# Attention with a key cache on one core: the second turn's keys transposed on TensorE, four steps of probabilities transposed by transfers, and a new order of all queues

## The chip, the cores and the metric

The kernel runs on one core of one Trainium2 chip. The metric is the device time of one execution in microseconds. A core has TensorE (matrix products, results into PSUM), VectorE and ScalarE (they copy out of PSUM and do the elementwise work), GpSimd (here only the identity matrix), and SyncE, which issues all transfers of this kernel, in one queue, SP: an instruction that waits there holds all that stand behind it.

## The reference

For 8 batches of 112 queries: q = x @ wq, with x of 8 x 112 x 640 and wq of 640 x 6144 (32 heads of 192); per batch and head scores = q @ k^T / sqrt(192) against 512 cached keys, p = softmax(scores), o = p @ v; then out = o @ wo, of 6144 x 640. All inputs and the output are bf16.

```
q = (x @ wq).reshape(B, Sq, H, Dh).transpose(0, 2, 1, 3)
scores = einsum("bhqd,bhkd->bhqk", q, k_cache) * Dh ** -0.5
p = softmax(scores)
o = einsum("bhqk,bhkd->bhqd", p, v_cache)
out = o.transpose(0, 2, 1, 3).reshape(B, Sq, H * Dh) @ wo
```

## The kernel before

The work goes in 16 turns: turn t takes one half of the heads (16) of one batch, first the lower half of all eight batches, then the upper. A turn has four steps of four heads; step n = 4t + s is the unit of softmax. Everything is unrolled, and the order on each engine is written out as text: `SP_WORK`, `PE_WORK`, `ACT_WORK`, `DVE_WORK`, one word an operation. `Plan.run` emits each list in its order, and before an operation waits for the semaphores of those it depends on (inputs ready, or a buffer or PSUM bank read out). So the order is fixed; only waits are found by the program.

The words on TensorE (the last number of most is the PSUM bank):

- X c: transposes of one chunk of 128 rows of x, five matmuls against the identity. K u: transposes of the keys of head u, six matmuls (line 477); the keys come untransposed as U lo.hi into `kn`, which lies in `wo_sb`. Before the change this is so in turn 0 alone; from turn 1 on K t on SP is one transfer of 3 MB that transposes on its way into `kt[t % 2]` (line 432). It waits until turn t - 2's scores have read that buffer.
- A m.lp and B m.lp: q for a pair of batches m and a pair of heads lp, two blocks (ten matmuls) and one block (five) of 224 columns (line 490). ScalarE copies them out (a, b) into places that `Q_PLACES` lists.
- S n: scores of step n (lines 521 to 538). VectorE makes the masked copies of q first (c, line 675), then scales and takes the maximum (m, line 685); ScalarE takes the exponent with its sum (e, line 695); VectorE inverts (r) and normalises (n, line 710).
- T n.j: transposes of p, eight matmuls (line 548), copied out by ScalarE (t n.0) and VectorE (t n.1). V n: the products with the values (lines 568, 581), copied out by ScalarE (v). `p_sb` holds two steps, so e of step n waits until p of step n - 2 has been read.
- O u.f.i: four matmuls each of o @ wo (line 597), added up by VectorE (p). In the last turns G (line 612) and L (line 627) take their place, and F (line 638) transposes the result of a batch, which ScalarE copies out (o) and Z stores.

On SP stand besides: X and W (x and wq), V t.lo (half a turn's values, 1.5 MB, two buffers and at the start a third in `wo_sb`), Y (wo), Z (stores). W of the upper half waits until q of the lower half has been made from the same columns; V waits until its buffer's last values were used.

## Time and profile before

| | us |
|---|---|
| median of three runs | 459.64 (459.57 to 460.03) |
| the profiled execution's own time | 460.54 |
| its span, first to last instruction | 458.7 |
| TensorE busy | 438.4 (96%) |
| VectorE busy | 360.8 (79%) |
| ScalarE busy | 347.3 (76%) |

The span is shorter than the execution's own time by what lies around the program. A group of instructions is named by its line, its engine and its tiles, output first. Busy time of TensorE runs to the modelled end of each matmul, and matmuls overlap, so the distance from one piece to the next tells more of their cost than their durations. The granted clock is the share of full speed that TensorE was given. For a transfer the view of a source line gives how long SP was held by its issue, the start of the issue, and the time from there to its landing.

### The profile page before, as it was taken

The page shows a single profiled execution, that of the slowest core. Times are in us where ns is not written, and L with a number is a line of the kernel's source. Part 1 is how long each engine was busy: PE and PEld are TensorE (multiplying, and loading weights), DVE is VectorE, ACT ScalarE, POOL GpSimd, SP SyncE. Part 2 cuts the span into 40 slices and gives each one's busy share as a digit, 9 for nine tenths or more (in the row PEclk, how much of TensorE's full clock was granted, in tenths as well). Part 3 has the DMA queues.
Part 4 walks back from the last instruction along what each step waited for, and adds up shares of the span by engine and source line. Part 5 has one row for each costly group of instructions (what it writes and reads, how often), then busy time and mean ns, then how long its engine had stood idle before and what let it go on. Part 6 is the DMA issues. An engine that isn't in the chain of part 4 may idle for free.

```text
span 458.7 us, 14942 instructions
## 1 busy us (share of the span) xinstructions
PE 438.4 (96%) x6307; PEld 399.2 (87%) x6307; DVE 360.8 (79%) x1165; ACT 347.3 (76%) x787; POOL 0.7 (0%) x6
## 2 busy tenths in 40 slices
PE   4999899999999999999999999997999999999996
...
PEclk9899999999999999999999999999999999999999
...
GB/s 278 372 350 224 241 327 352 237 306 287 260 215 247 362 275 214 308 243 331 206 337 209 309 235 326 300 189 368 225 274 260 281 287 261 219 253 222 178 14 51
DMA packets 234321, 119.63 MB, mean 261 GB/s; under 512 B 185744, under 2 KB 234256, under 8 KB 234256
## 3 DMA queue, kind: packets, MB, share of 16 engines
...
q14 instruction: 16, 0.13, 0.1%
HBM read 70.35 MB, written 1.15 MB: 156 GB/s over the span
## 4 chain that ended last, share of the span: by engine, by line
PE 87%; ACT 4%; DMA 4%; DVE 3%; issue 1%; SPq 0%; ACTq 0%
PE ps L490 18%; PE ps L597 17%; PE ps L581 12%; PE ps L548 10%; PE ps L536 7%; PE ps L568 7%; PE ps L521 6%; PE ps L523 6%; DMA wq_sb<-in_wq_dram 2%; ACT p_sb L695 2%; DMA vt<-in_v_cache_dram 2%; PE ps L612 1%; DVE s_sb L685 1%; PE ps L627 1%; ACT acc_q L650 1%
## 5 line engine op out<-in xcount | busy, mean ns | idle before, releaser
L695 ACT ACTIVATE p_sb<-s_sb,nmx 112x512 bf16<-112x512 f32 x256 | 183.1, 717 | 42.3 <-DVE s_sb L685 40.7
L685 DVE TENSOR_SCALAR_CACHE_REDUCE s_sb<-ps 112x512 f32<-112x512 f32 x256 | 172.9, 684 | 41.3 <-PE ps L538 16.9
L490 PE MATMUL ps<-xT_sb,wq_sb 128*128 128x224 bf16 x960 | 110.0, 262 | 2.7 <-DMA wq_sb<-in_wq_dram 0.9
L597 PE MATMUL ps<-oT_sb,wo_sb 128*128 128x224 bf16 x840 | 95.0, 259 | 0.8 <-ACT acc_q L650 0.4
L490 PEld LDWEIGHTS ps<-xT_sb,wq_sb 128*128 128x128 bf16 x960 | 88.6, 99 | 7.4 <-DMA wq_sb<-in_wq_dram 1.9
L710 DVE TENSOR_SCALAR p_sb<-p_sb,rinv 112x512 bf16<-112x512 bf16 x256 | 84.6, 349 | 3.2
L597 PEld LDWEIGHTS ps<-oT_sb,wo_sb 128*128 128x128 bf16 x840 | 77.1, 98 | 2.5 <-issue 0.7
L650 ACT ACTIVATE acc_q<-ps 128x224 bf16<-128x224 f32 (+1 forms) x128 | 55.9, 447 | 24.6 <-PE ps L490 19.8
L650 ACT ACTIVATE pT_sb<-ps 128x896 bf16<-128x896 bf16 x64 | 58.3, 911 | 13.0 <-PE ps L548 12.8
L548 PE MATMUL ps<-ident,p_sb 112*128 112x112 bf16 x1024 | 65.3, 213 | 0.1
L650 ACT ACTIVATE oT_sb<-ps 128x672 bf16<-128x672 f32 x64 | 46.5, 727 | 18.5 <-PE ps L581 16.2
L548 PEld LDWEIGHTS ps<-ident,p_sb 112*128 112x128 bf16 x1024 | 57.7, 98 | 2.5 <-DVE p_sb L710 0.7
L581 PE MATMUL ps<-pT_sb,vt 128*128 128x112 bf16 x992 | 59.5, 213 | 0.0
L581 PEld LDWEIGHTS ps<-pT_sb,vt 128*128 128x128 bf16 x992 | 49.8, 98 | 4.9
L695 ACT ACTIVATION_READ_ACCUMULATOR p_sb<-s_sb,nmx 112x1 f32 x256 | 49.2, 192 | 0.0
L650 DVE COPY pT_sb<-ps 128x896 bf16<-128x896 bf16 x64 | 39.7, 620 | 12.0 <-PE ps L548 11.2
L568 PEld LDWEIGHTS ps<-pT_sb,vt 128*64 128x64 bf16 x992 | 27.3, 109 | 16.8 <-ACT p_sb L695 7.2
L568 PE MATMUL ps<-pT_sb,vt 128*64 128x112 bf16 x992 | 36.2, 215 | 5.4 <-DVE p_sb L710 2.6
L521 PE MATMUL ps<-kt,acc_q 128*112 128x256 bf16 x128 | 35.2, 275 | 1.3 <-DVE kt L650 0.7
L523 PE MATMUL ps<-kt,acc_q 128*112 128x256 bf16 x128 | 34.9, 273 | 0.0
L521 PE MATMUL ps<-kt,qh 128*112 128x256 bf16 x128 | 34.9, 272 | 0.0
L523 PE MATMUL ps<-kt,qh 128*112 128x256 bf16 x128 | 34.9, 272 | 0.0
...
## 6 DMA issues: line engine op xcount, KB each, us to landing
...
wo_sb<-in_wo_dram SPq DMA_DIRECT2D x4, 1920.0 KB, 13.5
wq_sb<-in_wq_dram SPq DMA_DIRECT2D x7, 960.0 KB, 10.7
...
```

The source lines that it names most:

```text
L490: mm = e.matmul(ps[:, bank, j * S2:(j + 1) * S2], wq_sb[:, dc, c0:c0 + 128], xT_sb[:, dc, bp * S2:(bp + 1) * S2], start=(dc == 0), stop=(d ...
L521: e.matmul(ps[0:SQ, 2 * j, hs], ev, ktb[:, :, 0, cs(i)], start=(h == 0), stop=False, skip_group_check=True)
L523: mm = e.matmul(ps[0:SQ, 2 * j + 1, hs], od, ktb[:, :, 2, cs(i)], start=(h == 0), stop=False, skip_group_check=True)
L536: m1 = e.matmul(ps[0:SQ, 2 * j, hs], ev, ktb[0:64, :, 1, cs(i)], start=False, stop=True, skip_group_check=True)
L548: mm = e.transpose(psb[:, bank, c:c + SQ], p_sb[:, (4 * n + 2 * j + h) % 8, q * 128:(q + 1) * 128], ident[0:SQ, 0:SQ])
L568: mm = e.matmul(ps[64 * h:64 * h + 64, b0 + j, SQ:2 * SQ], vtb[:, h0 + 2 * j + h, d0:d0 + 64], pT(j, h, q), start=(q == 0), stop=(q == 3))
L581: mm = e.matmul(ps[:, b0 + j, 2 * h * SQ:(2 * h + 1) * SQ], vtb[:, h0 + 2 * j + h, d0:d0 + 128], pT(j, h, q), start=(q == 0), stop=(q == 3))
L597: mm = e.matmul(ps[:, bank, j * S2:(j + 1) * S2], wo_sb[:, KU * (u % 2) + k, m * 128:(m + 1) * 128], oT_sb[:, u % NO, k, :], start=(k == 0 ...
L650: return e.activation(dst, src, ACTF.Copy) if eng == "ACT" else e.tensor_copy(dst, src)
L685: return e.tensor_scalar(s_sb[:, a, :].rearrange("p (e c) -> p e c", e=2), ps[0:SQ, 2 * j:2 * j + 2, h * 256:(h + 1) * 256], -scale, None, ...
L695: return e.activation(p_sb[:, k, :], s_sb[:, a, :], ACTF.Exp, bias=nmx[:, k:k + 1], scale=-1.0, accum_out=rsum[:, k:k + 1])
L710: return e.tensor_scalar(p_sb[:, k, :], p_sb[:, k, :], rinv[:, k:k + 1], None, op0=ALU.mult)
```

## The change

Turn 1's keys are loaded untransposed too (U1.0.8 and U1.8.16, each once turn 0's keys have left those places of `kn`), and 16 more K words on TensorE transpose them; the copies go into `kt[1]`. The transposing transfer K1 is gone. K3, which takes `kt[1]` next, also waits for these copies.

D n products of the identity with itself (20 ahead of the first X, 8 ahead of the first A and B) go into a PSUM bank that nobody reads.

In steps 58 to 61 T and its two copies are gone. P n, a transfer on SP, transposes the four heads' p from `p_sb` into a part of `wq_sb` that is free once the last q has been made; V n reads it there, and e of step n + 2 waits for its landing instead of T.

The orders of all four lists and `Q_PLACES` are new: among others the head's transfers, Y0.1 now behind V2.0, V4.0 behind K5, W1.0.2 ahead of V5.0, W1.6.2 behind V7.0, Y1.0 behind V10.0, and the stores with Z2 behind Z6.

```diff
--- before.py
+++ after.py
@@ -17,238 +17,241 @@
...
 SP_WORK = """
-X0.0.2 W0.0.1 U0.4 W0.1.1 W0.2.2 X1.2.4 X2.4.7 U4.8 W0.6.2 W0.4.2 U8.16 V0.0 V0.8
-K1
-K2 V1.0 V1.8 Y0.0 V2.0
-K3 V2.8 Y0.1 V3.0
-K4 V3.8 V4.0
-K5 V4.8 W1.4.2 W1.2.2 V5.0 W1.0.2
+X1.2.4 X0.0.2 W0.1.1 W0.0.1 U0.0.4 W0.2.2 U0.4.8 W0.6.2 U0.8.16 W0.4.2 U1.0.8 X2.4.7 V0.0 V0.8 U1.8.16
+K2 V1.0 V1.8 Y0.0 V2.0 Y0.1
+K3 V2.8 V3.0
+K4 V3.8
+K5 V4.0 W1.2.2 V4.8 W1.4.2 W1.0.2 V5.0
 K6 V5.8 V6.0
-K7 V6.8 W1.6.2 V7.0
+K7 V6.8 V7.0 W1.6.2
 K8 V7.8 V8.0
 K9 V8.8 V9.0
-K10 V9.8 Y1.0 V10.0
+K10 V9.8 V10.0 Y1.0
 K11 V10.8 Y1.1 V11.0
 K12 V11.8 V12.0
 K13 V12.8 V13.0
 K14 V13.8 V14.0
-K15 V14.8 V15.0 V15.8 Z1 Z2 Z0 Z5 Z3 Z4 Z6 Z7
+K15 V14.8 P58 P59 V15.0 P60 P61 V15.8 Z3 Z0 Z1 Z4 Z6 Z2 Z5 Z7
 """
 PE_WORK = """
-X1.4 X0.6 A0.0.6 B0.0.4 K0.6 B0.1.5 A0.1.7 K2.3 K3.0 K1.2 A0.3.6 X2.5
-S0 A0.2.7 K6.0 B0.3.4 K5.5 X4.0 X3.1 X5.7 B0.7.6 B0.2.5 K7.2 K4.0 B0.6.7
-S1 B1.2.7 B1.3.6 B1.6.7 A0.6.6 K11.0 K8.1 A0.7.7 T0.0.4 K12.1 B0.5.6 X6.0 A0.4.7 K9.0 K15.3 A0.5.6 K10.5 B0.4.7 K13.4
-A1.6.6 B1.0.7 T0.1.5
...
-S44 V42.4 A6.2.6 A6.5.7 T43.0.4 T43.1.5
...
-S59 V57.4 O13.1.0.7 O13.1.1.7 O13.1.2.7 O13.1.3.7 F1.6 O13.1.4.7 O13.1.5.7 T58.0.4 T58.1.5 F2.6
-S60 V58.4 O12.2.0.7 O13.0.0.6 O12.2.1.7 O12.2.2.7 O13.0.1.6 O13.0.2.6 O13.2.0.7 O13.2.1.7 T59.0.4 T59.1.5 O13.2.2.7
-S61 V59.4 F0.6 G0.0.7 G0.1.7 G0.2.7 G1.0.6 G1.1.6 T60.0.4 G0.3.7 T60.1.5
-S62 V60.4 G1.2.6 G1.3.6 O13.3.0.7 O13.3.1.7 O13.3.2.7 T61.0.4 T61.1.5 F5.6
-S63 V61.4 G2.0.7 G2.1.7 G2.2.7 F4.6 G2.3.7 T62.0.4 T62.1.5 L0.0 V62.4 F3.6 T63.0.0 L1.0 T63.1.1 L0.1 L1.1 V63.2 L2.1
-L2.0 L3.0 L3.1 F6.5 F7.4
+D0.20.3 X3.5 X2.6 X1.4 X0.2 D1.8.3 B0.1.5 A0.1.6 A1.1.7 A0.0.6 B0.0.5 K0.0.1 K0.3.3 K0.2.0 K0.1.1 A1.0.6
+S0 B0.3.5 A0.2.6 B1.3.7 K0.5.5 B0.2.4 K0.4.0 A0.3.6 K0.6.1 B0.6.7 K0.7.6 A0.6.7
+S1 K0.11.5 A0.7.6 B0.7.7 T0.0.4 K0.12.5 K0.13.1 B0.4.7 A0.4.6 K0.10.0 B0.5.7 K0.8.1 K0.9.3 K1.1.0 K0.14.2 K0.15.4
+A0.5.6 X4.3 K1.5.4 X5.7 K1.7.2 T0.1.5 B1.0.6
+S2 V0.4 B1.6.7 K1.4.0 T1.0.4 T1.1.5 K1.2.6
+S3 V1.4 A1.6.7 K1.0.0 T2.0.4 K1.3.5 K1.10.1 A1.7.6 K1.6.7 T2.1.5 K1.8.6
+S4 V2.4 B1.2.6 K1.9.1 K1.11.0 A1.5.7 B1.7.6 X6.0 K1.14.2 B1.1.7 K1.12.3 K1.15.5 K1.13.4
+S5 A1.2.6 T3.0.4 A3.0.7 A2.0.6 T3.1.5
+S6 V3.4 A1.3.6 T4.0.4 T4.1.5 A3.7.7 B1.5.6 V4.4 A2.6.7 T5.0.4 T5.1.5
+S7 V5.4 A1.4.6 A2.5.7 B1.4.6 T6.0.4 T6.1.5
+S8 V6.4 A2.2.6 A3.3.7 T7.0.4 T7.1.5
...
+S40 B5.7.7 T38.1.5 O7.3.0.6 O7.3.1.6 B5.3.7 V38.4 A5.5.7 T39.0.4 O7.3.2.6 T39.1.5
+S41 V39.4 A6.1.6 T40.0.4 O7.0.0.7 T40.1.5 O7.0.1.7 O7.0.2.7 O8.3.0.6 O8.3.1.6 O8.3.2.6
...
+S43 V41.4 B6.0.7 O8.1.2.6 O8.1.3.6 O8.1.4.6 O8.1.5.6 A6.2.7 T42.0.4 T42.1.5
+S44 V42.4 B6.1.6 A6.0.7 T43.0.4 T43.1.5 A6.5.6
...
+S57 V55.4 O11.3.0.7 O11.3.1.7 O11.0.0.6 T56.0.4 O11.3.2.7 O11.0.1.6 O11.0.2.6 T56.1.5
+S58 V56.4 B7.7.6 O12.3.0.7 O12.3.1.7 O12.1.0.6 O12.1.1.6 O12.3.2.7 O12.1.2.6
+S59 F1.7 O12.1.3.6 O12.1.4.6 T57.0.4 O12.0.0.7 T57.1.5 O12.1.5.6 O12.0.1.7 O12.0.2.7 V57.4 F2.6
+S60 O13.1.0.7 O13.1.1.7 O13.0.0.6 O13.0.1.6 O13.0.2.6 O13.1.2.7 O13.1.3.7 O13.1.4.7 O12.2.0.6 O12.2.1.6 O13.1.5.7
+O12.2.2.6 V58.4 F3.7 O13.3.0.6 O13.3.1.6 O13.3.2.6 F0.7
+S61 V59.4 O13.2.0.7 O13.2.1.7 O13.2.2.7 G0.0.6 G0.1.6 G0.2.6 G0.3.6 G1.0.7
+S62 G1.1.7 G1.2.7 G1.3.7 G2.0.6 V60.4
+S63 F4.7 G2.1.6 G2.2.6 V61.4 G2.3.6 L0.0 T62.0.4 T62.1.5 L0.1 L1.1 T63.0.0 T63.1.1 V62.4 L1.0 V63.2 F6.4 L2.0 L3.0
+L2.1 L3.1 F5.7 F7.5
 """
 ACT_WORK = """
-x1 a0.0 b0.0 b0.1 a0.1 k1
-e0.0 a0.3 e0.1 e0.2 a0.2 b0.3 k5 b0.2 x3 k7 e0.3 b0.7 b0.6 b1.2 b1.3
...
-e63.0 v61 e63.1 t62.0 o4 e63.2 e63.3 v62 o3 t63.0 v63 o6 o7
+x3 x1 b0.1 a0.1 a0.0 b0.0 k0.1 a1.0 a1.1
+e0.0 b0.3 e0.1 a0.2 b0.2 b1.3 k0.5 a0.3 b0.6 k0.7 a0.6 e0.2 e0.3 k0.11
+e1.0 a0.7 b0.7 t0.0 b0.4 e1.1 k0.13 e1.2 a0.4 k0.9 b0.5 k0.15 k1.1 a0.5 e1.3 k1.7 k1.5 b1.0
+e2.0 v0 e2.1 t1.0 b1.6 e2.2 e2.3
+e3.0 v1 a1.6 e3.1 k1.3 e3.2 a1.7 t2.0 e3.3
+e4.0 b1.2 e4.1 k1.11 v2 a1.5 b1.7 e4.2 k1.9 k1.15 b1.1 e4.3 k1.13 a1.2
...
+e58.0 b7.7 e58.1 e58.2 e58.3 v56 o1
+e59.0 t57.0 e59.1 o2 e59.2 e59.3 v57
+e60.0 e60.1 o3 e60.2 v58 e60.3 o0
+e61.0 e61.1 v59 e61.2 e61.3
+e62.0 e62.1 e62.2 e62.3 v60 o4
+e63.0 e63.1 v61 e63.2 e63.3 t62.0 t63.0 v62 v63 o6 o5 o7
 """
 DVE_WORK = """
-x0 k0 k2 c0 k3
-m0.0 m0.1 x2 m0.2 k6 m0.3 x5 x4 c1 r0.0 k4
...
-m63.0 n62.1 r62.1 m63.1 n62.2 m63.2 n62.3 g2 r63.0 n63.0 t62.1 n63.1 m63.3 r63.1 n63.2 n63.3 t63.1 l0 l1
+x0 x2 k0.0 k0.3 k0.2 c0
+m0.0 m0.1 r0.0 m0.2 m0.3 k0.4 c1 k0.6 n0.0
+m1.0 m1.1 n0.1 r0.1 m1.2 m1.3 k0.10 n0.2 n0.3 k0.12 r1.0 n1.0 k0.14 k0.8 x4 c2 n1.1 x5 t0.1 r1.1 n1.2 n1.3
+m2.0 c3 m2.1 m2.2 k1.4 m2.3 t1.1 c4 r2.0
+m3.0 m3.1 n2.0 k1.2 n2.1 m3.2 r2.1 k1.0 k1.10 n2.2 n2.3 r3.0 c5 m3.3 t2.1 n3.0 k1.8 n3.1
...
+m59.0 m59.1 c60 r58.1 n58.2 t57.1 p12.1 m59.2 n58.3 r59.0 m59.3 n59.0 n59.1 p12.0 r59.1 n59.2 n59.3
+m60.0 p13.0 m60.1 c61 p12.2 p13.1 c62 m60.2 r60.0 n60.0 m60.3 n60.1 r60.1 n60.2
+m61.0 m61.1 n60.3 p13.3 m61.2 m61.3 c63 r61.0 p13.2 n61.0 n61.1 r61.1 n61.2 n61.3
+m62.0 g0 m62.1 m62.2 m62.3 g1 r62.0 n62.0 n62.1 r62.1
+m63.0 n62.2 m63.1 m63.2 m63.3 n62.3 g2 r63.0 n63.0 n63.1 r63.1 n63.2 n63.3 t62.1 t63.1 l0 l1
...
@@ -360,6 +363,7 @@
...
+        wq_flat = wq_sb[:].rearrange("p a b -> p (a b)")
         wo_flat = wo_sb[:].rearrange("p a b -> p (a b)")
...
@@ -375,14 +379,17 @@
...
         v_home = [0, 1, 2] + [(i + 1) % 2 for i in range(3, len(v_units))]
-        x_piece, wq_piece, kn_piece = {}, {}, {}
+        x_piece, wq_piece, kn_piece, by_dma = {}, {}, {}, []
         for kind, *a in work["SP"]:
+            if kind == "P":
+                by_dma.append(a[0])
             if kind == "X":
...
             elif kind == "U":
-                kn_piece.update({u: ("KN", *a) for u in range(*a)})
+                kn_piece.update({(a[0], u): ("KN", *a) for u in range(a[1], a[2])})
+        kn_turns = sorted({t for t, _ in kn_piece})
...
@@ -399,10 +406,11 @@
...
-        def load_kn(lo, hi):
-            def emit(e):
-                return e.dma_start(kn[:, lo:hi, :], k_cache[0, lo:hi].rearrange("u (r q) d -> r u (q d)", q=4))
-            add("SP", ("KN", lo, hi), [], emit, f"mKN{lo}", 16)
+        def load_kn(t, lo, hi):
+            def emit(e):
+                return e.dma_start(kn[:, lo:hi, :], k_cache[t, lo:hi].rearrange("u (r q) d -> r u (q d)", q=4))
+            old = [("KT", t - 1, u) for u in range(lo, hi)] if t else []
+            add("SP", ("KN", t, lo, hi), old, emit, f"mKN{t}_{lo}", 16)
...
@@ -421,7 +429,7 @@
...
             else:
-                old = [("KT", i) for i in range(HU)] + ([("PVm", 4, 1), ("PVm", 5, 1)] if u else [])
+                old = [("KT", *i) for i in kn_piece] + ([("PVm", 4, 1), ("PVm", 5, 1)] if u else [])
             add("SP", ("WO", half, u), old, emit, f"mWO{u}", 16)
...
@@ -431,6 +439,7 @@
...
             old = [("St", step_of(t - 2, s), 3) for s in range(4)] if t > 1 else []
+            old += [("evK", t - 2, u) for u in range(HU)] if t - 2 in kn_turns else []
             add("SP", ("K", t), old, emit, f"mK{t % 2}", 16)
...
@@ -445,13 +454,24 @@
...
             old = [("PVm", step_of(v_units[j][0], v_units[j][1] // 4 + s), 1) for j in old for s in range(2)]
-            old += [("KT", u) for u in range(HU)] if v_home[i] == 2 else []
+            old += [("KT", *i) for i in kn_piece] if v_home[i] == 2 else []
             add("SP", ("V", t, lo), old, emit, f"mV{v_home[i]}", 16)
...
             add("SP", ("OUT", b), [("oout", b)], emit, f"mOUT{b % DC}", 16)
+
+        def p_spare(n):
+            return wq_flat[:, by_dma.index(n) * 16 * SQ:(by_dma.index(n) + 1) * 16 * SQ].rearrange("p (c s) -> p c s", c=16)
+
+        def p_transposes(n):
+            k = 4 * n % 8
+
+            def emit(e):
+                return e.dma_start_transpose(p_spare(n), p_sb[:, k:k + 4, :].rearrange("p a c -> p (a c)"))
+            old = [d for m in range(NM // 2, NM) for lp in range(LP) for d in q_both(m, lp)]
+            add("SP", ("P", n), [("norm", n, i) for i in range(4)] + old, emit, f"mP{n % 2}", 16)
...
@@ -471,13 +491,21 @@
...
-        def k_transposes(u, bank):
+        def k_transposes(t, u, bank):
             def emit(e):
...
                 return mm
-            add("PE", ("KT", u), [kn_piece[u]], emit)
-            take(("KT", u), bank, ("KT", u), [("evK", u)])
+            add("PE", ("KT", t, u), [kn_piece[t, u]], emit)
+            take(("KT", t, u), bank, ("KT", t, u), [("evK", t, u)])
+
+        def idle_products(i, n, bank):
+            def emit(e):
+                for _ in range(n):
+                    mm = e.matmul(ps[:, bank, 0:128], ident[:, :], ident[:, :], start=True, stop=True)
+                return mm
+            add("PE", ("D", i), [], emit)
+            take(("D", i), bank, ("D", i), [])
...
@@ -523,7 +551,7 @@
...
                     return mm
-                add("PE", ("Sm", n, j), [("qc", n)] + ([("evK", 4 * s + i) for i in range(4)] if t == 0 else [("K", t)]),
+                add("PE", ("Sm", n, j), [("qc", n)] + ([("evK", t, 4 * s + i) for i in range(4)] if t in kn_turns else [("K", t)]),
                     emit)
...
@@ -558,7 +586,7 @@
...
             def pT(j, h, q):
-                return pT_sb[:, j, h, q * SQ:(q + 1) * SQ]
+                return p_spare(n)[:, 4 * (2 * j + h) + q, :] if n in by_dma else pT_sb[:, j, h, q * SQ:(q + 1) * SQ]
...
@@ -570,7 +598,8 @@
...
-            add("PE", ("PVt", n), [("evPT", n, 0), ("evPT", n, 1), ("V", t, 8 * (s // 2))], rests)
+            ready = [("P", n)] if n in by_dma else [("evPT", n, 0), ("evPT", n, 1)]
+            add("PE", ("PVt", n), ready + [("V", t, 8 * (s // 2))], rests)
             for j in range(2):
...
@@ -654,9 +683,9 @@
...
-        def ev_k(eng, u):
-            copy(eng, ("evK", u), [("KT", u)], kt[0][:].rearrange("p a m c -> p (a m) c")[:, :, u * 128:(u + 1) * 128],
-                 psb[:, bank_of["KT", u], 0:768].rearrange("p (c r) -> p c r", c=6))
+        def ev_k(eng, t, u):
+            copy(eng, ("evK", t, u), [("KT", t, u)], kt[t][:].rearrange("p a m c -> p (a m) c")[:, :, u * 128:(u + 1) * 128],
+                 psb[:, bank_of["KT", t, u], 0:768].rearrange("p (c r) -> p c r", c=6))
...
@@ -694,7 +723,8 @@
...
                                     accum_out=rsum[:, k:k + 1])
-            add(eng, ("exp", n, i), [("smax", n, i)] + ([("PT", n - 2, i // 2)] if n > 1 else []), emit)
+            old = [] if n < 2 else [("P", n - 2)] if n - 2 in by_dma else [("PT", n - 2, i // 2)]
+            add(eng, ("exp", n, i), [("smax", n, i)] + old, emit)
...
@@ -711,7 +741,8 @@
...
         def ev_pt(eng, n, j):
-            copy(eng, ("evPT", n, j), [("PT", n, j)] + ([("PVm", n - 1, j)] if n else []),
+            old = [("PVm", w, j) for w in range(n) if w not in by_dma][-1:]
+            copy(eng, ("evPT", n, j), [("PT", n, j)] + old,
                  pT_sb[:, j, :, :].rearrange("p h c -> p (h c)"), psb[:, bank_of["PT", n, j], 0:8 * SQ])
...
@@ -775,10 +806,11 @@
...
         bank_of = {(k + "T", *a[:-1]): a[-1] for k, *a in work["PE"] if k in "XK"}
-        loads = {"X": load_x, "W": load_wq, "U": load_kn, "V": load_v, "K": load_k, "Y": load_wo, "Z": store}
+        loads = {"X": load_x, "W": load_wq, "U": load_kn, "V": load_v, "K": load_k, "Y": load_wo, "Z": store,
+                 "P": p_transposes}
         for kind, *a in work["SP"]:
             loads[kind](*a)
-        on_pe = {"X": x_transposes, "K": k_transposes, "A": lambda *a: q_fill("a", *a), "B": lambda *a: q_fill("b", *a),
+        on_pe = {"D": idle_products, "X": x_transposes, "K": k_transposes, "A": lambda *a: q_fill("a", *a), "B": lambda *a: q_fill("b", *a),
                  "S": scores, "T": transposes, "V": values, "O": o_sums, "G": o_six, "L": o_last, "F": o_final}
...
```

336 lines of the change are left out of this document (155 added, 181 removed), and 16 rows, old and new, of the table Q_PLACES.

## The prediction

> **What bounds the kernel now.** I read the page first (shares, slices), then a table of stretches, then the order of the instructions at the head and at the one dip in the middle, then single transfers.
>
> ```profile
> span 458.7 us, 14942 instructions
> PE 438.4 (96%) x6307; PEld 399.2 (87%) x6307; DVE 360.8 (79%) x1165; ACT 347.3 (76%) x787; POOL 0.7 (0%) x6
> ...
> PE   4999899999999999999999999997999999999996
> ...
> PEclk9899999999999999999999999999999999999999
> ```
>
> TensorE is the bound nearly everywhere; what it loses lies in the first slices, at one dip (slice 28) and at the end. The stretches say how much (columns: length, busy time of PE, PEld, DVE, ACT, POOL, granted clock, DMA share, GB/s):
>
> ```profile
> 0.00:16.30 16.30, 9.77 (x79) 8.31 (x80) 2.79 (x7) 4.80 (x8) 0.70 (x6) 0.90 0.91 305
> 16.30:73.30 57.00, 53.79 (x713) 47.71 (x711) 39.43 (x124) 43.98 (x103) 0.00 (x0) 1.00 1.17 302
> 73.30:312.00 238.70, 235.36 (x3388) 214.46 (x3386) 204.75 (x665) 189.86 (x435) 0.00 (x0) 1.00 1.16 273
> 312.00:318.00 6.00, 3.40 (x56) 2.92 (x54) 4.04 (x14) 3.18 (x10) 0.00 (x0) 1.00 1.06 374
> ...
> 432.40:455.00 22.60, 22.29 (x417) 20.64 (x414) 14.24 (x46) 14.62 (x31) 0.00 (x0) 1.00 0.20 67
> 455.00:458.70 3.70, 0.00 (x0) 0.00 (x0) 0.00 (x0) 0.68 (x1) 0.00 (x0) 1.00 0.26 78
> ...
> 8.30:11.70 3.40, 1.53 (x17) 1.11 (x15) 0.56 (x1) 0.55 (x2) 0.00 (x0) 1.00 1.06 382
> 11.70:15.10 3.40, 3.40 (x29) 3.08 (x28) 1.00 (x3) 0.90 (x2) 0.00 (x0) 0.50 1.07 370
> ```
>
> To 16.3, where the scores of step 0 begin, PE works 9.8 of 16.3 us, and from 11.7 to 15.1, after a stretch with 1.53 us of work in 3.4, its clock is halved. The last 3.7 us hold no matmul. The dip at 312 loses 2.6 us.
>
> **The price of one word of the order.** Matmuls overlap, so I price by the distance to the next piece, as the chain of waits gives it (start, us, what):
>
> ```profile
> 2.32 8.65 DMA wq_sb<-in_wq_dram
> ...
> 29.49 0.67 PE ps L477 x12
> 30.16 0.96 PE ps L490 x10
> ...
> 39.89 0.51 PE ps L568 x16
> 40.41 0.89 PE ps L581 x16
> ...
> 423.92 0.79 PE ps L548 x16
> ```
>
> A key transpose of one head (K, six matmuls) is 0.67 / 2 = 0.34 us; A is 0.96 and B, half of it, 0.48; V is 0.51 + 0.89 = 1.40; T is 0.79 / 2 = 0.40; O, four matmuls of A's width, 0.38; a matmul of G or L I price like one of T, 49 ns.
>
> **TensorE work.** Added: 16 K, 16 x 0.34 = +5.4 us. Removed: two T in each of steps 58 to 61, 8 x 0.40 = -3.2 us. The 20 + 8 identity products I cost at nothing: their cover is the wait for the first transfers, below; without it, at half clock (183 ns for 224 columns, below, so some 0.1 us for 128) they would cost 2.8. Net +2.2 us, on the bound engine: the change must win that back from waits.
>
> **Head, to the scores of step 0.** The rows (start, us, then what; behind them single transfers, by issue time and by time to landing):
>
> ```profile
> 5.88 2.75 PE L490 MATMUL ps<-xT_sb,wq_sb 128*128 128x224 bf16 x15 [0.63 <-DVE xT_sb L650]
> ...
> 14.64 0.33 DVE L675 COPY qh<-acc_q 64x672 bf16<-64x672 bf16 x1
> ...
> 15.24 0.55 DVE L650 COPY kt<-ps 128x768 bf16<-128x768 bf16 x1
> ...
> 16.35 0.27 PE L521 MATMUL ps<-kt,acc_q 128*112 128x256 bf16 x1
> ...
> 73.38 0.28 PE L521 MATMUL ps<-kt,acc_q 128*112 128x256 bf16 x1
> ...
> L411 SPq DMA_DIRECT2D wq_sb<-in_wq_dram x1: 1074/1074/1074, 2.9 to 2.9; - x1
> DMA to landing us min/median/max: 10.7/10.7/10.7
> ```
>
> By the shapes, 320 + 480 + 768 + 480 = 2048 KB are queued up to the piece that lands at 2.32 + 8.65 = 10.97, and the next 960 KB land at 2.9 + 10.7 = 13.6: 2.64 us more. In the new order the last piece that step 0 needs, the keys U0.0.4, has 320 + 320 + 480 + 480 + 768 = 2368 KB up to it, so it lands at 10.97 + 320 / 960 x 2.64 = 11.9. Then one K (0.34), three copies of keys on VectorE (3 x 0.55) and the two copies of qc (2 x 0.33), with some 0.2 for handing over: S0 at 14.8 instead of 16.35. Up to there the new order has done 4 X, 4 A, 2 B, 4 K, the old 3 X, 3 A, 2 B, 4 K: 0.96 + 0.28 (an X is five transposes at 56 ns) = 1.24 us more. The gain is 1.55 + 1.24 = 2.8 us. Bounds: 1.2, if the keys land so late that S0 stays at 16.35; 4.3, if they land with the 2048 KB at 10.4 and hand over at once.
>
> The 15 matmuls at 5.88 took 2.75 us, against 0.96 for ten later on, or 1.44 for fifteen: half clock, 1.3 us; the halved stretch lost 1.7 more. The Trainium skill, page "TensorE: Matmul & The Clock Gate", section "Part 1: The HAM clock gate", says that the clock is halved by default, is released after one busy window of about 3.4 us, and comes back halved after an idle one; the trace agrees, with 0.50 for 3.4 us behind a poor window. By that rule alone, identity products from 1.5 us on would save 1.3 + 1.7 = 3.0 us. I don't add this to the 2.8: with the full clock PE waits for the same pieces, so the row of the transfer decides; by the rule the sum would be 0.2 lower.
>
> **S0 to S7 (16.35 to 73.38, 57.0 us).** By the prices above and 1.54 for an S (the start of one to the next word), the old order has 7 S, 17 A, 16 B, 12 K, 4 X, 12 T, 5 V: 51.7 us, so 5.3 are waits and stretching. The new has 7 S, 15 A, 13 B, 28 K, 3 X, 12 T, 5 V: 53.4 us. What it queues in front (X0 to U1.8.16, 320 x 2 + 960 x 4 + 480 + 768 x 2 + 1536 x 5 = 14176 KB) would land at 10.97 + (14176 - 2048) / 960 x 2.64 = 44.3; the K that needs its last piece stands 5 us behind S3, which comes 7.7 + 11.4 + 4.9 us of work and some 2 of waits after S0: near 46. So transfers stay just ahead, with under 2 us of margin; that is the cover, and beyond it each us late is a us of stall. The copies of the 16 heads fall on engines with room on average:
>
> ```profile
> L650 ACT ACTIVATE kt<-ps 128x768 bf16<-128x768 bf16 x7 | 5.7, 811 | 2.0 <-PE ps L477 2.0
> L650 DVE COPY kt<-ps 128x768 bf16<-128x768 bf16 x9 | 5.0, 553 | 11.3 <-PE ps L477 11.2
> ...
> L650 ACT ACTIVATE acc_q<-ps 128x448 bf16<-128x448 f32 x64 | 34.2, 539 | 11.1 <-PE ps L490 9.4 <-PE ps L538 1.5
> L650 ACT ACTIVATE acc_q<-ps 128x224 bf16<-128x224 f32 x64 | 22.3, 354 | 13.5 <-PE ps L490 10.3 <-PE ps L538 2.6
> ```
>
> ScalarE gets 8 x 0.81 and loses 3 x 0.54 + 3 x 0.35 and one X copy (0.7): 43.98 + 3.1 = 47.1 us; VectorE 39.43 + 8 x 0.55 - 0.5 = 43.4. I keep the 5.3 us of waits (bounds 3.2, PE's idle time in the stretch, and 9.3, worked out below). S7 then begins at 14.8 + 53.4 + 5.3 = 73.5, where it began before, with 0.8 us less work left.
>
> **From S7 on.** The work left falls from 375.5 to 374.7. The old order spends 454.95 - 73.38 - 375.5 = 6.1 us of waits here. The largest:
>
> ```profile
> 316.30 0.58 PE L568 MATMUL ps<-pT_sb,vt 128*64 128x112 bf16 x16 [2.60 <-DVE p_sb L710]
> ...
> L445 SPq DMA_DIRECT2D vt<-in_v_cache_dram x1: 582/582/582, 307.1 to 307.1; - x1
> DMA to landing us min/median/max: 9.1/9.1/9.1
> ...
> L432 SPq DMA_TRANSPOSE kt<-in_k_cache_dram x1: 24274/24274/24274, 282.7 to 282.7; - x1
> DMA to landing us min/median/max: 26.3/26.3/26.3
> ```
>
> The releaser named had long been done; the values V10.8, issued at 307.1 behind the 24.3 us that the transposing K11 holds SP, land at 316.2. That is the wait. Between the end of S39, which frees K11's buffer, and V42 the new order has two more A: 35.1 us of work for 33.2. Against it stands Y1.0, now queued after V10.0, directly ahead of K11. I take 1.3 of the 2.6 us off (bounds 0 and 2.6) and leave the other waits: 374.7 + 6.1 - 1.3 = 379.5.
>
> The other moves on SP I cost at nothing. V4.0 stands behind K5 now: with the 12.7 us that a lone K holds SP and 7.1 for lone values (both rows below) it lands 19.8 us after S15 for a V16 that is 23.5 us of work away; if K5 takes K11's 24.3, it is late by 8. K6 is needed 25.9 us of work after S19, 30.1 before, but W1.0.2 ahead of it is released by B3.1 before S19 and no longer after S20.
>
> **Tail.** The nearest rows to a transposing transfer of p (112 x 2048, 448 KB) are K2, alone in the queue, and the last values:
>
> ```profile
> L432 SPq DMA_TRANSPOSE kt<-in_k_cache_dram x1: 12657/12657/12657, 46.4 to 46.4; - x1
> DMA to landing us min/median/max: 16.3/16.3/16.3
> ...
> L445 SPq DMA_DIRECT2D vt<-in_v_cache_dram x1: 368/368/368, 428.0 to 428.0; - x1
> DMA to landing us min/median/max: 7.1/7.1/7.1
> ```
>
> 448 / 3072 of 12.7 is 1.9 us of SP, plus 16.3 - 12.7 = 3.6: 5.5 us to landing (bounds 3.6, and 26.3 if a small one takes as long as K11). Queued behind the waits for p: V15.0 behind P59, V15.8 behind P61, all stores. P61 starts when step 61 is normalised, about the start of S62; V15.8 lands 1.9 + 7.1 = 9.0 later, and V62 stands 12.7 us of work behind that start. P60 has some 7 us between its p and V60. P58 also gates the exps of step 60, with nearly no slack, but those have 2.6 us before they matter. So the transfers cost nothing, up to about 2.5 us more than I price. One store is worse placed: Z2 stands behind Z6 and must land before the last output copy; with o5 now between o6 and o7 I add 0.3.
>
> Sum: 73.5 + 379.5 + 0.3 + 3.7 = 457.0 for the span, against 458.7: -1.7. The profiled execution took 460.54, 0.9 above the median of the runs (459.64); on the median the change gives 458.0.
>
> **Rivals.** *VectorE and ScalarE become the bound from S0 to S7* (slower). They do in 57.0 us what they are given at 77% and 69%; at the same shares 47.1 us need 61.0 and 43.4 need 62.7, for my 58.7. That is 2.3 to 4.0 us more, 460.3 to 462.0; I put it at 461.6. It ends slower once the stretch passes 61.3. For it: the copies aren't spread, 11 of the 28 lie between S1 and S2 and 6 between S4 and S5. Against: both engines sit idle in the stretch for 13 us or more. 22%.
>
> *The head's gain is only a shift* (no change): the keys land late, S0 stays at 16.35, gain 1.2 instead of 2.8: 459.6. For it: the old order's first 768 KB of keys took 7.8 us to land against 4.1 for the weights before them. 17%.
>
> ```profile
> L404 SPq DMA_DIRECT2D wo_sb<-in_k_cache_dram x1: 517/517/517, 1.8 to 1.8; - x1
> DMA to landing us min/median/max: 7.8/7.8/7.8
> ```
>
> *Transfers of p as slow as K11* (26.3 us): V58 and V60 would each come some 13 us late, 484. Against it: K2 moved seven times as much in 16.3. 3%. The Trainium skill, page "VectorE: DVE Perf Modes", section "The three transpose paths", gives 1309 ns for a 128x128 block by transfer; sixteen blocks in turn would be an estimated 21 us. The trace disagrees for streams: 96 blocks in 16.3.
>
> **Numbers.** Forecast 458.0, 58%, own range 455.0 (3.2 us of waits to S7, the dip gone) to 458.7. 0.2% (0.9 us) is about what a measurement tells from no change. Faster 0.58, same 0.17, slower 0.22 + 0.03 = 0.25. The range 455.0 to 462.0 takes in the first two rivals and leaves out the third.
>
> **What would show it.** Full granted clock from about 5 us and no halved stretch; S0 near 14.8, S7 near 73.5; 56 ns per key transpose; V62 and V60 without waits on transfers; V42 waiting 1.3 us or less. Wrong if S7 comes past 76, if PE waits on keys in S1 to S4, or if a P takes over 8 us.

## The result and the profile after

The changed kernel takes 452.6 us (median; 451.79 to 453.83) where the kernel before, on the same chip, takes 459.6 (457.88 to 460.03). The ratio is 0.9857, with a 95% interval of 0.9823 to 0.9891: 7.0 us less. The forecast was 458.0, with a range down to 455.0: the sign was right, and the gain is some four times the one forecast. The profiled execution took 451.79, its span is 450.0. It lies below its median, and that of the kernel before (460.54) above its own: the two spans differ by 8.7 us, the medians by 7.0, so the stages below add up to 1.7 us more than the gain.

From the page of the changed kernel: busy time of TensorE, then its busy tenths and its granted clock in 40 slices.

```profile
span 450.0 us, 15075 instructions
...
PE 440.4 (98%) x6367; PEld 402.6 (89%) x6367; DVE 361.1 (80%) x1169; ACT 347.9 (77%) x791; POOL 0.7 (0%) x6
...
PE   6999999999999999999999999999999999999996
...
PEclk9999999999999999999999999999999999999999
```

The dip of slice 28 is gone, and so are the 8 of TensorE's fifth slice and the 8 of the clock's second. TensorE is busy 2 us longer in a span that is 8.7 us shorter. The stretches (columns as in the prediction):

```profile
0.00:15.05 15.05, 11.45 (x123) 10.62 (x123) 3.10 (x8) 5.58 (x10) 0.70 (x6) 1.00 0.87 293
15.05:70.40 55.35, 54.66 (x767) 49.46 (x768) 42.94 (x133) 48.46 (x108) 0.00 (x0) 1.00 1.07 326
308.00:314.00 6.00, 5.97 (x91) 5.38 (x89) 5.03 (x16) 4.71 (x10) 0.00 (x0) 1.00 1.07 367
396.70:446.60 49.90, 49.65 (x808) 45.33 (x805) 36.30 (x122) 32.77 (x72) 0.00 (x0) 1.00 0.76 181
446.60:450.00 3.40, 0.00 (x0) 0.00 (x0) 0.00 (x0) 0.71 (x2) 0.00 (x0) 0.95 0.28 84
```

Between S0 (15.04) and S7 (70.40) TensorE idles 0.7 us, where it idled 3.2; around S44 it idles 0.03 us, where it idled 2.6. Stage by stage, with the word prices of the prediction (work) and what is left over (called waits; it holds stretching too), in us:

| stage | before: length = work + waits | after: length = work + waits |
|---|---|---|
| to S0 | 16.35 | 15.04 |
| S0 to S7 | 57.03 = 51.69 + 5.34 | 55.35 = 53.40 + 1.95 |
| S7 to S58 | 331.85 = 326.23 + 5.62 | 326.28 = 325.85 + 0.43 |
| S58 to the last matmul | 49.72 = 49.23 + 0.49 | 49.90 = 48.85 + 1.05 |
| after it | 3.8 | 3.4 |

Of the 8.7 us, 1.3 lie ahead of S0, 1.7 between S0 and S7 (although 1.7 of work were added there), 5.6 between S7 and S58, and nothing at the end: the new order has moved work behind S58 for the T that it lost.

From S7 to S58 the two kernels differ in nothing but their orders. The whole lists of what TensorE waited for there (sum, times, longest), first before, then after:

```profile
PE ps L568 <- DVE p_sb L710: 2.6, 1, 2.6
PE ps L568 <- ACT acc_q L650: 0.8, 1, 0.8
PE ps L568 <- ACT p_sb L695: 0.6, 1, 0.6
PE ps L568 <- ACT pT_sb L650: 0.5, 1, 0.5
PE ps L597 <- ACT acc_q L650: 0.4, 1, 0.4
PE ps L490 <- DVE acc_q L735: 0.3, 1, 0.3
PE ps L568 <- DMA vt<-in_v_cache_dram: 0.3, 1, 0.3
PE ps L597 <- issue: 0.3, 1, 0.3
PE ps L568 <- DVE pT_sb L650: 0.3, 1, 0.3
```

```profile
PE ps L596 <- DMA vt<-in_v_cache_dram: 0.7, 2, 0.4
PE ps L576 <- DVE p_sb L740: 0.4, 1, 0.4
PE ps L518 <- DVE acc_q L766: 0.2, 1, 0.2
```

The nine waits sum to 6.1 us, the four that are left to 1.3. Besides the dip, all entries for ScalarE are gone: V (L568, now L596) and O (L597) waited for its work in four places, 2.3 us in all. Two late values (0.7 us), a T that waits for p and an A that waits for its bank are left.

One price flatters both columns. V is priced at 1.40 us, but takes 1.31 wherever nothing waits behind it (325.11 to 326.43 in the second execution of the kernel before). With 51 V from S7 to S58, both waits there are 4.4 us too low, 10.0 and 4.8; their difference stands.

### The profile page after: what moved, and what is told of

It reads as the page before. It is cut to its first block, busy times and chain, and to the rows that moved or that the text cites. A ratio compares the mean times of both kernels' runs of the same rounds, so it can differ in the third digit from the quotient of the medians.

```text
span 450.0 us, 15075 instructions
## 1 busy us (share of the span) xinstructions
PE 440.4 (98%) x6367; PEld 402.6 (89%) x6367; DVE 361.1 (80%) x1169; ACT 347.9 (77%) x791; POOL 0.7 (0%) x6
## 4 chain that ended last, share of the span: by engine, by line
PE 87%; DMA 5%; DVE 3%; ACT 3%; issue 1%; SPq 0%; ACTq 0%
PE ps L518 17%; PE ps L626 17%; PE ps L610 12%; PE ps L576 10%; PE ps L564 7%; PE ps L596 7%; PE ps L549 6%; PE ps L551 6%; DMA vt<-in_v_cache_dram 4%; PE ps L497 2%; DVE s_sb L714 2%; DMA wq_sb<-in_wq_dram 1%; PE ps L656 1%; PE ps L641 1%; ACT p_sb L724 1%; ACT acc_q L679 1%
## 5 line engine op out<-in xcount | busy, mean ns | idle before, releaser
L518 PE MATMUL ps<-xT_sb,wq_sb 128*128 128x224 bf16 x960 | 107.5, 259 | 2.2 <-DMA wq_sb<-in_wq_dram 1.8
L626 PE MATMUL ps<-oT_sb,wo_sb 128*128 128x224 bf16 x840 | 93.4, 259 | 0.0
L679 ACT ACTIVATE pT_sb<-ps 128x896 bf16<-128x896 bf16 x60 | 54.5, 909 | 10.4 <-PE ps L576 8.1
L576 PE MATMUL ps<-ident,p_sb 112*128 112x112 bf16 x960 | 61.4, 213 | 0.5 <-DVE p_sb L740 0.4
L679 ACT ACTIVATE oT_sb<-ps 128x672 bf16<-128x672 f32 x64 | 46.3, 723 | 14.9 <-PE ps L610 14.2
L576 PEld LDWEIGHTS ps<-ident,p_sb 112*128 112x128 bf16 x960 | 54.3, 98 | 2.4 <-DVE rinv L733 0.7
L610 PE MATMUL ps<-pT_sb,vt 128*128 128x112 bf16 x928 | 55.7, 213 | 0.0
L610 PEld LDWEIGHTS ps<-pT_sb,vt 128*128 128x128 bf16 x928 | 46.5, 98 | 4.5
L679 DVE COPY pT_sb<-ps 128x896 bf16<-128x896 bf16 x60 | 37.1, 619 | 9.3 <-PE ps L576 7.0
L596 PEld LDWEIGHTS ps<-pT_sb,vt 128*64 128x64 bf16 x928 | 25.4, 109 | 11.2 <-issue 6.3
L596 PE MATMUL ps<-pT_sb,vt 128*64 128x112 bf16 x928 | 33.9, 216 | 0.8 <-DMA vt<-in_v_cache_dram 0.7
```

Of the source, the lines that this page charges most:

```text
L518: mm = e.matmul(ps[:, bank, j * S2:(j + 1) * S2], wq_sb[:, dc, c0:c0 + 128], xT_sb[:, dc, bp * S2:(bp + 1) * S2], start=(dc == 0), stop=(d ...
L576: mm = e.transpose(psb[:, bank, c:c + SQ], p_sb[:, (4 * n + 2 * j + h) % 8, q * 128:(q + 1) * 128], ident[0:SQ, 0:SQ])
L596: mm = e.matmul(ps[64 * h:64 * h + 64, b0 + j, SQ:2 * SQ], vtb[:, h0 + 2 * j + h, d0:d0 + 64], pT(j, h, q), start=(q == 0), stop=(q == 3))
L610: mm = e.matmul(ps[:, b0 + j, 2 * h * SQ:(2 * h + 1) * SQ], vtb[:, h0 + 2 * j + h, d0:d0 + 128], pT(j, h, q), start=(q == 0), stop=(q == 3))
L626: mm = e.matmul(ps[:, bank, j * S2:(j + 1) * S2], wo_sb[:, KU * (u % 2) + k, m * 128:(m + 1) * 128], oT_sb[:, u % NO, k, :], start=(k == 0 ...
L679: return e.activation(dst, src, ACTF.Copy) if eng == "ACT" else e.tensor_copy(dst, src)
```

## The experiments

Two theories. **Orders**: the waits belonged to the old orders of TensorE, ScalarE and VectorE, and the new orders take them away, whichever of the parts are in. **Parts**: the untransposed keys, the identity products and the transfers of p take them away by themselves. A third possibility is **chance**: single late transfers of one profiled execution. The runs come from several chips; each ratio is to the kernel before on the same chip.

### One part taken out of the changed kernel

The identity products alone (nobody reads them, so all that the reference asks for is still computed):

```diff
-D0.20.3 X3.5 X2.6 X1.4 X0.2 D1.8.3 B0.1.5 ...
+X3.5 X2.6 X1.4 X0.2 B0.1.5 ...
```

> The new kernel without its 28 identity products, nothing else changed. Theory of the parts: TensorE is at half clock for one or two stretches of 3.4 us more, but the head is set by the landing of the first keys at 11.9, so S0 comes at 15.5 to 17 instead of 15.04 and the time grows by 0.5 to 2 us (453 to 454.6). Rival, the clock alone counts: 3.0 us more (455.6). Rival, the new orders are everything: no change (452.6).

Measured: 455.86, 0.9932 of the kernel before (0.990 to 0.9965). S0 comes at 16.22 (16.68 in the other execution of new orders without the products, the last of this section); in the six profiled executions with them it comes at 13.5 to 15.0, on average 14.2. S0 is as the first expectation has it, the time as the second. The timeline of TensorE and the durations of the matmuls of A and B, first without the products, then with them (a second execution of the changed kernel; start, us):

```profile
3.98 2.29 PE L488 MATMUL ps<-ident,oT_sb 128*128 128x128 bf16 x20 [3.98 <-DMA oT_sb<-in_x_dram]
7.27 5.95 PE L518 MATMUL ps<-xT_sb,wq_sb 128*128 128x224 bf16 x36 [1.00 <-DMA wq_sb<-in_wq_dram]
...
L518 PE MATMUL ps<-xT_sb,wq_sb x25: 369/394/394, 7.3 to 11.7; 128*128 128x224 bf16 x25
...
L518 PE MATMUL ps<-xT_sb,wq_sb x15: 259/259/263, 12.1 to 14.9; 128*128 128x224 bf16 x15
```

```profile
3.72 2.31 PE L488 MATMUL ps<-ident,oT_sb 128*128 128x128 bf16 x20
5.83 0.86 PE L505 MATMUL ps<-ident 128*128 128x128 bf16 x8
7.59 4.01 PE L518 MATMUL ps<-xT_sb,wq_sb 128*128 128x224 bf16 x40 [0.91 <-DMA wq_sb<-in_wq_dram]
...
L518 PE MATMUL ps<-xT_sb,wq_sb x40: 259/259/270, 7.6 to 11.3; 128*128 128x224 bf16 x40
```

Forty matmuls of A and B take 4.01 us with the products, 36 take 5.95 without, 2.3 more than at the pace of the forty. The column of the granted clock shows 1.00 for both, but the durations say otherwise: without the products 25 of them last about 394 ns, up to 11.7 us, and from 12.1 us on they last 259. So the head ran at a lower clock until about 12 us, and that is worth the 2.0 us by which S0 moves, not the 3.0 that the prediction worked out by the rule in the Trainium skill ("TensorE: Matmul & The Clock Gate", "Part 1: The HAM clock gate"). The trace agrees with the rule that a busy stretch of some 3.4 us gives the full clock: with the products TensorE is busy for 3.39 of the 3.40 us from 1.5 us on, and all 40 matmuls from 7.6 us on last 259 ns. The transfers hold the rest, as the prediction argued.

Of the remaining 1 us or so of the 3.3, this profiled execution shows a part at another place: V54 waited 1.8 us, and from 391.0 to 394.4 the granted clock was 0.50. Of the twelve runs, the four with a mean granted clock of 0.999 or 1.000 took 454.2 to 454.9 us, some 2 above the changed kernel; the other eight took more. Why they do is open.

p of steps 58 to 61 back on TensorE, first with T58 directly behind S60, then with the copies v57 and v58 put ahead of two exps:

```diff
-K15 V14.8 P58 P59 V15.0 P60 P61 V15.8 ...
+K15 V14.8 V15.0 V15.8 ...
-S60 O13.1.0.7 ...
+S60 T58.0.4 T58.1.5 O13.1.0.7 ...
```

> The new kernel with p of steps 58 to 61 transposed on TensorE again (8 T and their 8 copies back in the orders, no P transfers). Theory of the parts: TensorE is the bound to the end, so the 3.2 us of work come back whole: 455.8. Rival: the transfers and what stands behind them had cost as much as the work saved: 452.6.

> The new orders with p of steps 58 to 61 transposed on TensorE again, and this time v57 and v58 copied ahead of two exps, so that the eight T don't wait for a bank as they did (2.3 us between S60 and S61). If the transfers save just the removed work, the time is 452.6 + 8 x 0.40 = 455.8. If it stays near 459, the transposes cost more than their own time in this order, because their copies also load ScalarE and VectorE.

Measured: 459.09 (ratio 0.9987, 0.9964 to 1.001), beyond both expectations, and with the better place 456.67 (0.9955, 0.9927 to 0.9982), 4.4 us above the changed kernel beside it (452.27). In the first, T58 waited for the bank that v57 had still to read out (2.3 us between S60 and S61). In the second, S58 to the last matmul is 53.58 for 49.77: TensorE is busy 3.2 us longer (52.78 for 49.55), as priced, and waits 0.6 more. The 8 x 0.40 = 3.2 us are right. What they cost in an order depends on whether the banks come free in time.

Turn 1's keys by the transposing transfer K1 again:

```diff
-... U1.0.8 X2.4.7 V0.0 V0.8 U1.8.16
+... X2.4.7 V0.0 V0.8 K1
```

> The new kernel with turn 1's keys loaded by one transposing transfer K1 behind V0.8, without the 16 K words and their copies. Theory of the parts: 5.4 us of TensorE work go, but S4, which would then start near 44.2, waits for K1, which can't land before about 50.5 (V0.8 at 36, plus the 14.6 us that K1 took behind V0.8 before); net 1 us slower (453.8), with a wait of some 6 us at S4. Rival, the untransposed load only adds work: 5 us faster (447.5).

Measured: 457.13 (0.9942, 0.9914 to 0.9971). The list of TensorE's waits from 40 to 60 us, and the transfer:

```profile
PE ps L549 <- DMA kt<-in_k_cache_dram: 7.9, 1, 7.9
```

```profile
L440 SPq DMA_TRANSPOSE kt<-in_k_cache_dram x1: 25574/25574/25574, 23.3 to 23.3; - x1
...
DMA to landing us min/median/max: 28.8/28.8/28.8
```

K1, issued at 23.3, lands at 52.1, and S4 begins at 52.12. The changed kernel begins S4 at 47.55. The 16 K cost 5.4 us and take away a wait of 8. The run is slower than either expectation because the wait costs more than its length: behind it TensorE ran at half clock up to 55.3 us (granted clock 0.50 from 48.5 on), with 3.2 us of busy time at that clock, some 1.6 us lost.

All three undone, the new orders alone:

> The new orders alone: no identity products, T in steps 58 to 61, K1 as one transposing transfer, all as before, but every other word in the new order. Theory of the orders: the new orders hold most of the 7 us, so 453 to 455.5. Theory of the parts: the three parts hold it, so 457.5 to 460.

Measured: 462.04, slower than before (1.0068, 1.0034 to 1.0101) and than either expectation. But its waits are not those of the old order: 0.36 us from S0 to S1 (before: 2.27), 0.00 from S5 to S7 (1.59), 1.2 from S7 to S58 (5.6). It loses 8.3 us between S3 and S5, where S4 waits 4.8 us for K1 and the half clock follows, as in the run with K1, and 2.3 by the badly placed T58. The new orders have little work ahead of S4 to cover K1: they were made for keys that don't come by it.

### The kernel before again

> The kernel before again, for a second profiled execution of the same orders. If its waits belong to its orders, the second trace has them at the same places: about 2.3 us between S0 and S1, 1.6 between S5 and S7, 1.9 between S20 and S30, 2.6 between S44 and S50, about 6.1 from S7 on. If the 2.6 us ahead of V10.8 (or any other) was one late transfer of that one execution, it is missing here and the waits from S7 on are 3.5 or less. The time is the same either way, 459.6.

Measured: 458.92 (ratio 1.0, 0.9974 to 1.0025). The profiled execution was the longest of its eleven (462.60, span 460.8). S0 came at 14.18 instead of 16.35, with the same kernel: weights landed 0.7 us earlier (A and B go on at 10.29 instead of 11.02), and the stretch from 11.7 to 15.1, halved in the execution that the prediction read, has the full clock here, as it has in the four other executions of old orders, where S0 comes at 14.0 to 14.9. And this is what became of the 2.2 us (S4, in the timeline of TensorE):

```profile
51.16 0.29 PE L547 MATMUL ps<-kt,acc_q 128*112 128x256 bf16 x1 [1.61 <-DMA kt<-in_k_cache_dram]
```

S4 waited for K1's landing (at 51.0). In five executions of the old order with K1, S0 lies between 14.0 and 16.4, and S4 between 50.8 and 51.6. In the execution that the prediction read it is the same, but hidden: K1 lands at 23.8 + 26.6 = 50.4, and S4 began at 51.57.

```profile
L432 SPq DMA_TRANSPOSE kt<-in_k_cache_dram x1: 22501/22501/22501, 23.8 to 23.8; - x1
...
DMA to landing us min/median/max: 26.6/26.6/26.6
```

The waits from S7 on came back at the same places, the copies to 0.1 us and the transfers by other amounts, 8.6 us in all from S7 to S58. How much of this is chance is worked out below from all executions.

### One part alone in the old orders

The identity products:

> The old orders with the 28 identity products alone. If the clock decides the head also in the old order: full clock by about 6 us, no halved stretch at 11.7, S0 at 14.7 to 15.2 instead of 16.35, and the gain stays to the end: 458.1 to 458.5. If the first transfers decide (X2.4.7 lands at 13.6) and the later waits take the rest back, S0 comes within 0.5 us of 16.35 and the time stays within 0.4 of 459.6.

Measured: 457.16 (0.9978, 0.9956 to 1.0001), about 1 us, not clear of no change. S0 at 13.96, hardly earlier than in the other old executions with the full clock, and S1 at 25.18, as before: a K waited 2.0 us for a late piece of turn 0's keys, 3.4 us at a granted clock of 0.50 followed, and K1, landing at 51.2, would have held S4 in any case (it came at 51.53).

The transfers of p:

```diff
-K15 V14.8 V15.0 V15.8 Z1 ...
+K15 V14.8 P58 P59 V15.0 P60 P61 V15.8 Z1 ...
-S59 V57.4 ... T58.0.4 T58.1.5 F2.6
+S59 V57.4 ... F2.6
```

> The old orders with one part of the change: p of steps 58 to 61 transposed by transfers, their eight transposes and copies taken out, nothing else moved. If a transposing transfer of p takes the 4.0 to 5.9 us to landing of the new trace and nothing waits for it, the gain is the whole of the removed work, 8 x 0.40 = 3.2 us: 456.4. If the old order gives it too little room (V58 stands directly behind S60, some 6 us behind the last exp of step 58; in the new order there are O pieces between), V58 to V60 wait 0.5 to 2 us each and the gain is 0 to 1.5: 458 to 459.6.

Measured: 469.88, 11 us slower (1.0247, 1.0212 to 1.0283), far outside both expectations. The four transfers, here and in the changed kernel, and TensorE's waits from 405 us on, here:

```profile
L470 SPq DMA_TRANSPOSE wq_sb<-p_sb x4: 1523/1533/4679, 413.2 to 435.8; - x4
...
  PE ps L594: 5.8, 3
...
DMA to landing us min/median/max: 4.0/4.1/8.6
```

```profile
L472 SPq DMA_TRANSPOSE wq_sb<-p_sb x4: 1517/1528/1697, 408.8 to 425.9; - x4
...
DMA to landing us min/median/max: 4.0/4.7/5.9
```

```profile
PE ps L594 <- DMA wq_sb<-p_sb: 5.8, 3, 2.5
PE ps L665 <- ACT xT_sb L677: 3.0, 2, 2.8
```

Three of the four transfers are as quick, but the old order has no work but S60's 1.5 us between the words of step 59 and V58: V58, V59 and V60 all wait. Behind P60 and P61 on SP stand V15.8 and the first three stores; an output copy waits 4.9 us for one of them to empty its place, and F (L665) for the bank of that copy. From S58 to the last matmul TensorE idles 10.1 of 63.0 us and is busy 52.9 for 46.1 of priced work: the other 6.8 us are half clock (13.6 us at a granted clock of 0.50, behind the waits). The new order puts twelve O ahead of V58, and V58 to V61 have 2.0 to 3.1 us to spare.

The untransposed keys:

```diff
-... U8.16 V0.0 V0.8
-K1
+... U8.16 U1.0.8 V0.0 V0.8 U1.8.16
...
-S4 V2.4 B2.4.7
+S4 V2.4 K1.6.6 K1.7.7 K1.8.0 K1.9.1 K1.10.2 K1.11.3 K1.12.6 K1.13.7 K1.14.4 K1.15.5 B2.4.7
```

The six other K stand in S2 and S3; two A there use another bank, and some copies were moved to make room.

> The old orders with turn 1's keys untransposed and transposed on TensorE, the 16 K between S2 and S4, nothing else. If the new orders took the waits away, not the keys, the old order's 2.3 us ahead of S1, 0.7 ahead of S5 and 1.6 ahead of S7 stay and the 16 x 0.34 = 5.4 us come on top, less the wait for K1 ahead of S4 (0.3 to 2.1 us): S7 at 75.5 to 77.0, 462.0 to 464.0. If untransposed keys take those waits away by themselves, S7 comes at 72 to 74 and the time is 459 to 460.5.

Measured: 467.88 (1.0205, 1.0151 to 1.0258), beyond either expectation. From S0 to S7 it has 12.9 us of waits, the largest for these:

```profile
PE ps L494 <- ACT kt L676: 2.5, 2, 2.3
PE ps L494 <- ACT acc_q L676: 2.2, 2, 1.8
PE ps L515 <- ACT kt L676: 1.7, 1, 1.7
```

K and A (L494, L515) wait for banks that ScalarE's copies have not left. It looks like the rival of the prediction, VectorE and ScalarE as the bound from S0 to S7, but ScalarE is busy 21.7 of the 31.5 us from S2 to S5, 69%: with the 16 K where I put them, its copies stand in the wrong places, and its sum of work is no limit. Half clock adds to it here too (0.50 from 53.2 to 56.6).

### The wait ahead of V10.8

The first run moves Y1.0 behind V10.0 in the old orders, the second ahead of it in the new ones. The edit of the first:

```diff
-K10 V9.8 Y1.0 V10.0
+K10 V9.8 V10.0 Y1.0
```

> The old orders with one word moved: Y1.0 behind V10.0 instead of ahead of it, as in the new order. If the wait ahead of V10.8 comes from what is queued ahead of K11, it changes here: 1.3 us less of the 2.6 or, if Y1.0 is better there, all of it, 457.0 to 458.3. If the wait comes from when S39 and V40 stand in TensorE's order, or from chance, moving Y1.0 alone does nothing: 459.6, with the wait as often as in the kernel before.

> The new orders with Y1.0 ahead of V10.0 again, as in the old order. If Y1.0 directly ahead of K11 is what keeps V10.8 in time, a wait of 1 to 4 us ahead of V42 (between S44 and S45) comes back: 453.6 to 456.6. If the place of S39 and V40 in TensorE's order decides, nothing changes: 452.6, and V42 waits less than 0.5 us.

Measured: old orders 463.26 (1.009, 1.0055 to 1.0126), outside its expectations, new orders 452.35 (0.9861, 0.9813 to 0.9909), as without the edit. In the old orders the first O of turn 8 now waited for Y1.0 itself:

```profile
PE ps L624 <- DMA wo_sb<-in_wo_dram: 6.2, 1, 6.2
```

That delay hides what the move did to V42, so this run settles nothing about it. In the new orders V42 waits for nothing with Y1.0 in either place: there its place doesn't matter. K11 and V10.8 in the changed kernel:

```profile
L440 SPq DMA_TRANSPOSE kt<-in_k_cache_dram x1: 22945/22945/22945, 277.2 to 277.2; - x1
```

```profile
L454 SPq DMA_DIRECT2D vt<-in_v_cache_dram x1: 582/582/582, 300.2 to 300.2; - x1
...
DMA to landing us min/median/max: 7.5/7.5/7.5
```

V10.8 lands at 307.7, and V42 comes at 309.57: 32.4 us behind K11's issue, where the old order comes after 33.6, 2.6 of them the wait. So TensorE's order gives V10.8 1.4 us more (the two A of the prediction), and in this execution the two transfers took 3.0 us less (22.9 and 7.5 for 24.3 and 9.1). The second part is luck: in the other executions they take 29.7 to 33.7 us in the old orders and 29.2 to 33.2 in the new ones. V10.8's landing holds V42 in three of five executions of the old orders (before, again, with D) and in one of eight of the new ones (with K1).

### The changed kernel again

> The changed kernel again, for a second profiled execution. If its few waits belong to its orders, the word prices give again some 2.0 us of waits from S0 to S7 and 0.4 to 1.3 from S7 to S58, against 5.3 to 7.9 and 2.9 to 8.6 in four executions of the old orders. If the first profiled execution was a lucky one, waits of 3 us or more show up from S7 on. Time 452.6 +- 0.8.

Measured: 452.27 (0.9869, 0.9811 to 0.9927), span 449.6; waits of 2.95 us from S0 to S7 and 0.1 from S7 to S58. The time is as expected; in S0 to S7 a K waited 0.7 us for its keys. With all profiled executions together, the waits from S7 to S58, where only orders differ:

| orders | executions | waits S7 to S58, us | mean |
|---|---|---|---|
| old | before, before again, with P, with D, with K | 5.6, 8.6, 2.9, 3.6, 3.1 | 4.8 |
| new | after, after again, Y1.0 moved, without D, T (both), K1, orders alone | 0.4, 0.1, 1.0, 3.3, 1.1, 0.3, 0.4, 1.2 | 1.0 |

(The old orders with Y1.0 moved, 11.6, have a wait of their own and are left out.) That is 3.8 us on average. With V at 1.31, and the smallest excess of each piece over its price taken as what returns in every execution:

| orders | total | returns in all | the rest: lowest, mean, highest |
|---|---|---|---|
| old (five) | 9.1 | 5.1 | 2.1, 4.0, 7.8 |
| new (eight) | 5.3 | 3.1 | 1.3, 2.2, 4.5 |

So 1 to 2 of the 3.8 us (1.1 to 2.0 with any five of the eight new ones) belong to the orders: the same waits at the same places in every execution, as the 1.0 us ahead of V20 in all five of the old ones. The rest differs from execution to execution, much of it late transfers and the half clock behind a wait. It is smaller in the new orders, but that this is the orders' doing is shown only in part, by the 1.4 us of room for V10.8.

## Why the prediction was wrong, point by point

**The work: right.** "Net +2.2 us": by the same prices all words of the changed kernel come to 435.4 us against 433.2. T undone lengthens TensorE's busy time by 3.2, and the stage with eleven of the new K, S3 to S5, takes 15.8 us for 15.0 of work. The identity products cost nothing: X begins at 3.72 and 3.91 us with them and at 3.98 without, and behind them A and B still wait 0.9 us or more for weights. Only V was priced wrong, 1.40 for 1.31; there are 64 in both kernels, so the net stands.

**Head: right as a place, wrong as a gain.** S0 at 14.8: it came at 15.04, with U0.0.4 landing at 11.94 (forecast 11.9), and at 13.5 to 14.7 in other executions; within that spread the hit is luck. The 16.35 that it was compared with was one execution's, the only one of the old orders with the clock halved from 11.7 to 15.1; the old kernel begins S0 at 14.2 as well. And the view of single transfers held a fact that I overlooked: K1's landing at 50.4, 1.1 us ahead of S4. With K1 in the queue no more than that of a gain at the head passes S4. To take this floor away is what the 16 K buy.

**"I keep the 5.3 us of waits" (S0 to S7): the first failed step.** They measured 1.95 (2.95 in the second execution), below the lower bound of 3.2. That bound was the old order's idle time, so it too took the old order for the new one. S7 came at 70.40, not 73.5: all of the 3.1 us are this term, as the start and the work came out as forecast. I had carried over the remainder of the old order to a stage whose order was new from end to end. Two places make up all of it: 2.3 us between S0 and S1 and 1.6 ahead of S7 go with the new orders even without any of the parts (0.36 and 0.00 there). The K that might have waited for U1.8.16 did not: it landed at 44.52 (forecast 44.3).

**"... and leave the other waits" (S7 on): the second failed step.** Forecast 4.8, measured 1.5 from S7 to the last matmul. The dip at V42 went whole: 2.6, of which I took 1.3; the two A gave 1.4, and shorter transfers, which is luck, the rest. The entries for ScalarE went too, 2.3 us, which I had not asked about at all. Each was in the list of waits of before, with its place; each could have been followed into the new order by asking which words now stand between the copy and the matmul that needs it. Y1.0, which I set against the A, makes no difference in the new orders. The stages of the two traces overstate the gain by 1.7 us, as said; the repeated executions leave 1 to 2 us from S7 to S58 that are the orders' for sure.

**Tail: right.** P held SP for 1.5 us and landed after 4.0 to 5.9 (forecast 1.9 and 5.5); V58 to V61 had 2.0 to 3.1 us to spare, V15.8 1.0; the stage behind the last matmul is 3.4 us for 3.7 + 0.3. That the transfers "cost nothing" is true of the new order alone: in the old one they cost 11 us.

**The rivals.** The bound by VectorE and ScalarE did not come, at 42.94 and 48.46 us of work (forecast 43.4 and 47.1) in 55.35: they were busy 78% and 88% of the stage, so the shares of before, 69% and 77%, were no limit. In the old order, with the same number of K, waits for ScalarE's copies came at a share of 69%: the place of each copy decides. The head as a shift was half true, by K1. The range reached down to 455.0 by way of "3.2 us of waits to S7, the dip gone"; it kept the other waits even at its lower end (by these terms that end is 454.6), and S0 to S7 went below the 3.2 too.

What stays open: 1 us or so of what the identity products are worth, how much of the varying waits from S7 on the new orders prevent, and which single word of the new orders removes which wait, as the orders were only tried whole.
